# Chunked attention followed by a gated MLP: softmax weights written as block-diagonal 128x128 tiles, V products on the whole of TensorE in blocks 2 to 8

## The chip, the cores and the metric

The kernel runs on one core of a Trainium2 chip. The metric is the device time of one execution in microseconds (us), lower is better. Every comparison of times is between executions in the fast state (b_again, a single run whose state is unknown, serves for its profile alone), and a kernel is always timed in turns with the kernel before on the same chip. A ratio is the mean time of one kernel's fast runs over that of the other's of the same rounds, so it is not quite the ratio of the medians that are quoted beside it.

TensorE is written PE in the profile (PEld is its weight load), VectorE DVE, ScalarE ACT, GpSimd POOL and SyncE SP. A "q" after an engine's name is its instruction queue, for instance ACTq for a DMA that ScalarE issues.

## The reference, cut to what matters

```python
# q, k, v: (8, 8, 576, 64) float32; chunks of 64 tokens, 9 chunks per sequence
scores = (q_c @ k_c.transpose(...)) / sqrt(64)      # 64x64 per chunk and head
attn   = softmax(scores)
out    = attn @ v_c                                 # 64x64 @ 64x64
x      = out as (4608, 512)
h      = x @ w_in                                   # (512, 2048)
g      = h * sigmoid(beta * h)
result = g @ w_out                                  # (2048, 512)
```

The 4608 tokens are worked on in nine blocks of 512, numbered 0 to 8. Attention is 64x64 work per head and chunk; the two large products are 128x512 matmuls, 128 of them per block.

## The kernel before

All instructions are put into queues by a small scheduler: `at(time, function, ...)` gives an order, in slots of four 128x512 matmuls, and semaphores are derived from what is read and written. For blocks 2 to 8 the attention of the next block runs inside the w_out products (`mm2`) of the block before it. An attention starts at slot T, and the block's first w_in product (`mm1`) is at slot T + 16.

```python
def exp(blk, bank):                      # bank: a PSUM bank with 512 scores per partition
    dst, src = E[:, bank, :], A[:, bank, :]
    ...
    P.op("act", lambda e: e.activation(dst, src, AF.Exp, scale=0.125), ...)

def attend(blk, m, u, ps, bank):         # m: 128 tokens, u: half of the heads
    ...
    for h in range(4 * u, 4 * u + 4):
        for c2 in range(2):              # two chunks, two 64x64 quarters of TensorE
            r = slice(64 * c2, 64 * c2 + 64)
            ... e.matmul(ps[r, bank, 128 * (h % 4):128 * (h % 4) + 65],
                         E[r, e0 + h % 2, col:col + 64], vaug[r, m, h, 0:65])

def normalize(blk, m, us, ps, bank): ...  # DVE: reciprocal of column 64, then multiply, into x_sb
def turn_x(blk, m):                       # DMA transpose, issued by SyncE
    P.dma("sp", lambda e: e.dma_start_transpose(xT[:, :, 128 * m:128 * m + 128], x_sb[:, m, :]), ...)

def attention(blk, T):
    for u in range(2):
        at(T + 0.6, scores, blk, u)
    for i in range(4):
        at(T + 1 + 0.1 * i, exp, blk, i)
    for j in range(2):
        for m in (2 * j, 2 * j + 1):
            for u in range(2):
                at(T + 4.1 + 2.5 * j, attend, blk, m, u, A, 2 * (m % 2) + u)
            at(T + 4.2 + 2.5 * j, normalize, blk, m, (0, 1), A, 2 * (m % 2))
            at(T + 4.3 + 2.5 * j, turn_x, blk, m)
```

`mm1` reads all four turns (m = 0 to 3) of a block, so the last of them to land decides when a block's first w_in matmul can start.

The softmax here doesn't subtract the row's maximum and nothing guards it: scores larger than these inputs give would overflow.

## Time and profile before

| | before |
|---|---|
| median of the first three runs | 294.89 us (294.52 to 295.69) |
| span of the profiled execution | 293.6 us |
| PE / ACT / DVE / POOL busy | 96% / 51% / 48% / 25% |
| period from one block's scores to the next's | 29.95 us |

The first and the fourth part of the page of before: busy us and share of the span of each engine, and the chain of waits that ended last by engine.

```profile
PE 282.8 (96%) x2417; PEld 139.2 (47%) x2453; DVE 140.2 (48%) x231; ACT 148.4 (51%) x235; POOL 74.0 (25%) x109
PE 92%; DMA 2%; DVE 2%; ACT 2%; issue 1%; ACTq 0%; DVEq 0%
```

TensorE is busy 96% of the time, and 92% of the chain is TensorE. Matmuls are pipelined, so "busy" alone would not prove a limit; the chain does. Here is the chain of before through block 5, in order of time (start, length, what):

```profile
155.98 0.86 PE F L504 x4
156.84 0.74 PE A L394 x64
157.59 0.16 issue
157.75 3.40 PE F L504 x15
161.15 0.63 PE A L415 x32
161.78 0.54 PE F L504 x2
162.31 0.05 issue
162.37 1.24 PE F L504 x5
163.61 0.63 PE A L415 x32
164.24 2.70 PE F L504 x12
166.93 0.05 issue
166.99 5.13 PE F L504 x23
172.11 1.08 PE F L460 x5
```

L394 are the scores, L415 the V products, L504 w_out and L460 w_in. No other engine is on it. The short "issue" pieces come from matmul records that are missing in the trace (15 of 16, 7 of 8), not from waits. The timeline of TensorE in the same place:

```profile
159.69 1.46 PE L504 MATMUL F<-w_out_bf,g 128*128 128x512 bf16 x6
161.07 0.70 PE L415 MATMUL A<-vaug,E 64*64 64x65 bf16 x32
161.71 1.90 PE L504 MATMUL F<-w_out_bf,g 128*128 128x512 bf16 x7
```

A length in the timeline includes the tail of the last matmul. Costs below are therefore taken from start to start in the trace: 128x512 matmuls start every 0.2157 us. From the start of the last one ahead of a V burst to the start of the next one behind it is 0.94 us, so a burst costs 0.94 - 0.216 = 0.725 us, and two of them 1.45 us a block.

### The profile page before, as it was taken

What the parts mean: (1) busy time and instruction counts of PE and PEld (TensorE: products, weight loads), DVE (VectorE), ACT (ScalarE), POOL (GpSimd) and SP (SyncE); (2) the same over time, 40 slices, a digit from 0 to 9 for tenths busy, and PEclk for the clock granted to TensorE, in tenths of its full rate; (3) what the DMA queues carried; (4) which work ended last, traced back from release to release, by engine and by line L of the source; (5) the groups of instructions that cost most, each with busy time, mean ns of one, the idle gap of its engine ahead of it and who ended that gap; (6) DMA issues with size and microseconds to landing.
All of it is one profiled execution on the core that took longest, in us unless ns stands there. A gap on an engine that the chain in (4) does not pass through costs nothing.

```text
span 293.6 us, 5823 instructions
## 1 busy us (share of the span) xinstructions
PE 282.8 (96%) x2417; PEld 139.2 (47%) x2453; DVE 140.2 (48%) x231; ACT 148.4 (51%) x235; POOL 74.0 (25%) x109
## 2 busy tenths in 40 slices
PE   7799999999999999999999999999999999999994
PEld 3554456745444544454444444454444444544441
DVE  0657536784247333834373427442844175408600
ACT  2567425784167515851486057704861387137511
POOL 1346753514231503152032303230234000000000
PEclk9799999999999999999999999999999999999999
DMA  6999999999799959999998599959999920340033
GB/s 235 259 359 399 405 287 295 240 204 278 148 269 246 223 115 269 263 201 193 213 262 171 143 216 239 194 125 194 199 177 202 200 57 0 80 136 2 0 71 71
DMA packets 133497, 57.53 MB, mean 196 GB/s; under 512 B 116576, under 2 KB 124768, under 8 KB 133472
## 3 DMA queue, kind: packets, MB, share of 16 engines
q1 hardware_dynamic: 127872, 47.20, 72.7%
q10 hardware_dynamic: 5600, 9.97, 10.7%
q8 instruction: 19, 0.31, 0.5%
q14 instruction: 6, 0.05, 0.1%
HBM read 36.71 MB, written 9.44 MB: 157 GB/s over the span
## 4 chain that ended last, share of the span: by engine, by line
PE 92%; DMA 2%; DVE 2%; ACT 2%; issue 1%; ACTq 0%; DVEq 0%
PE F L504 42%; PE F L460 40%; PE A L415 3%; DMA kstage<-in_k_dram 2%; PE A L394 2%; PE F L480 1%; ACT tt L490 1%; PE F L452 1%; PE A L350 1%; PE F L350 1%; DVE kcast L266 0%; DVE x_sb L427 0%; PE F L443 0%; ACT xT L264 0%; PE F L415 0%
## 5 line engine op out<-in xcount | busy, mean ns | idle before, releaser
L472 DVE SCALAR_TENSOR_TENSOR g<-tt,F 128x512 bf16<-128x512 bf16 x136 | 93.4, 687 | 78.2 <-ACT tt L469 77.9
L504 PE MATMUL F<-w_out_bf,g 128*128 128x512 bf16 x550 | 127.2, 379 | 2.1 <-issue 1.1
L460 PE MATMUL F<-xT,w_in_bf 128*128 128x512 bf16 x534 | 118.2, 379 | 0.5
L469 ACT ACTIVATE tt<-F,beta_half 128x512 bf16<-128x512 f32 x136 | 93.5, 687 | 24.5 <-PE F L460 24.2
L504 PEld LDWEIGHTS F<-w_out_bf,g 128*128 128x128 bf16 x576 | 54.4, 98 | 63.0 <-POOL w_out_bf L266 0.2
L460 PEld LDWEIGHTS F<-xT,w_in_bf 128*128 128x128 bf16 x544 | 53.2, 98 | 64.0 <-DVE g L472 0.5
L512 ACT ACTIVATE ostage<-F 128x512 f32<-128x512 f32 x34 | 20.3, 597 | 88.6 <-PE F L504 88.2
L266 POOL CAST qcast<-qstage 128x1024 bf16<-128x1024 f32 (+1 forms) x18 | 17.0, 945 | 72.7 <-DMA qstage<-in_q_dram 72.7
L266 POOL CAST vaug<-vstage 128x512 bf16<-128x512 f32 x36 | 21.9, 613 | 47.8 <-DMA vstage<-in_v_dram 32.9
L427 DVE TENSOR_TENSOR x_sb<-A,rden 128x512 bf16<-128x512 f32 x34 | 23.5, 691 | 1.2
L266 POOL CAST kcast<-kstage 128x512 bf16<-128x512 f32 (+1 forms) x29 | 18.2, 628 | 23.2 <-DMA kstage<-in_k_dram 23.1
L425 DVE RECIPROCAL rden<-A 128x8 f32<-128x8 f32 x34 | 6.9, 202 | 35.2 <-PE A L415 35.2
L404 ACT ACTIVATE E<-A 128x512 bf16<-128x512 f32 x28 | 14.5, 603 | 4.4 <-PE A L394 4.4
L415 PEld LDWEIGHTS A<-vaug,E 64*64 64x64 bf16 x544 | 10.3, 108 | 6.9 <-ACT ostage L512 3.0
L415 PE MATMUL A<-vaug,E 64*64 64x65 bf16 x544 | 12.5, 193 | 0.0
L266 POOL CAST w_in_bf<-wstage 128x1024 bf16<-128x1024 f32 (+1 forms) x8 | 7.8, 987 | 5.5 <-DMA wstage<-in_moe_w_in_dram 5.5
L266 POOL CAST w_out_bf<-wstage 128x1024 bf16<-128x1024 f32 x8 | 8.1, 1041 | 2.1 <-DMA wstage<-in_moe_w_out_dram 2.1
L480 PE MATMUL F<-xT,w_in_bf 128*128 128x256 bf16 x64 | 7.9, 273 | 0.7 <-DVE xT L266 0.5
L490 ACT ACTIVATE tt<-F,beta_half 128x256 bf16<-128x256 f32 x16 | 6.4, 496 | 1.2 <-PE F L480 1.2
L494 DVE SCALAR_TENSOR_TENSOR g<-tt,F 128x512 bf16<-128x512 bf16 x8 | 5.5, 687 | 2.8 <-ACT tt L490 2.6
L266 DVE CAST qcast<-qstage 128x1024 bf16<-128x1024 f32 x2 | 1.9, 936 | 10.4 <-DMA qstage<-in_q_dram 10.4
L480 PEld LDWEIGHTS F<-xT,w_in_bf 128*128 128x128 bf16 x64 | 5.9, 98 | 1.7 <-DVE xT L266 0.9
(50 smaller groups left out, 68.8 us busy)
## 6 DMA issues: line engine op xcount, KB each, us to landing
vstage<-in_v_dram SPq DMA_DIRECT2D x32, 256.0 KB, 5.0
out_dram<-ostage ACTq DMA_DIRECT2D x32, 256.0 KB, 4.0
kstage<-in_k_dram SPq DMA_DIRECT2D x30, 256.0 KB, 7.1
qstage<-in_q_dram SPq DMA_DIRECT2D x12, 512.0 KB, 6.0
wstage<-in_moe_w_out_dram SPq DMA_DIRECT2D x4, 1024.0 KB, 14.5
qstage<-in_q_dram SPq DMA_DIRECT2D x8, 256.0 KB, 9.4
wstage<-in_moe_w_in_dram SPq DMA_DIRECT2D x4, 512.0 KB, 7.4
wstage<-in_moe_w_in_dram SPq DMA_DIRECT2D x2, 1024.0 KB, 11.8
```

Of the source, the lines that this page charges most:

```text
L266: P.op(eng, lambda e: e.tensor_copy(dst, src), reads=r, writes=wr)
L404: P.op("act", lambda e: e.activation(dst, src, AF.Exp, scale=0.125), reads=[K("A", bank, v=("s", blk))], writes=[K("E", bank, v=blk)])
L415: return e.matmul(ps[r, bank, 128 * (h % 4):128 * (h % 4) + 65], E[r, e0 + h % 2, col:col + 64], vaug[r, m, h, 0:65])
L425: P.op("dve", lambda e: e.reciprocal(rd, o[:, :, :, 64]), reads=r, writes=[K("rden", m, u, v=blk) for u in us])
L427: P.op("dve", lambda e: e.tensor_tensor(x_sb[:, m, 256 * us[0]:256 * (us[0] + n)].rearrange("p (b h d) -> p b h d", h=4, b=n), o[:, :, :, ...
L460: P.op("pe", lambda e, c=c: e.matmul(F[:, bank, :], w_in_bf[:, c, 256 * e0 + i:256 * e0 + 256:2], xT[:, c, :], start=(c == 0), stop=(c == ...
L469: P.op("act", lambda e: e.activation(tt[:, T % NTT, :], F[:, bank, :], AF.Tanh, scale=beta_half[:, e0, i:i + 1]), reads=[K("F", bank, v=(" ...
L472: P.op("dve", lambda e: e.scalar_tensor_tensor(g2[:, t, :], tt[:, T % NTT, :], 1.0, F[:, bank, :], ALU.add, ALU.mult), reads=[K("F", bank, ...
L480: P.op("pe", lambda e, i=i, c=c: e.matmul(F[:, bank, 256 * i:256 * i + 256], w_in_bf[:, c, 256 * pair + i:256 * pair + 256:2], xT[:, c, 25 ...
L490: P.op("act", lambda e, i=i: e.activation(tt[:, s, 256 * i:256 * i + 256], F[:, bank, 256 * i:256 * i + 256], AF.Tanh, scale=beta_half[:, ...
L504: P.op("pe", lambda e, t=t: e.matmul(F[:, s, :], g2[:, t, 128 * s:128 * s + 128], w_out_bf[:, t, :], start=(t == 0), stop=(t == NT - 1)), ...
L512: f = (lambda e: e.activation(dst, src, AF.Copy, scale=0.5)) if eng == "act" else \
```

## The change

The intent is to use all rows and columns of TensorE. exp writes the two 64x64 weights of two chunks onto the diagonal of a 128x128 tile whose other quarters were cleared once (in a staging buffer that is free by then). One 128x65 matmul then takes the place of two 64x65 matmuls in opposite quarters. Because exp must now write to different columns for the upper and lower 64 partitions, each exp covers 64 partitions by 1024 columns instead of 128 by 512. The schedule is changed with it: four bursts of 8 products, first half of the heads first, instead of two bursts of 32.

```diff
-        def exp(blk, bank):
-            dst, src = E[:, bank, :], A[:, bank, :]
+        EB = wstage[:, 0, :].bitcast(BF16).rearrange("k (g x) -> k g x", x=128)
+        def clear_E():
+            P.op("pool", lambda e: e.memset(EB, 0.0), ...)
+        def exp(blk, u, c2):
+            r = slice(64 * c2, 64 * c2 + 64)
+            dst = EB[r, 16 * u:16 * u + 16, 64 * c2:64 * c2 + 64]
+            src = A[r, 2 * u:2 * u + 2, :].rearrange("k b x -> k (b x)")
             ... 
+        def attend_pairs(blk, m, u, bank):
+            for h in range(4 * u, 4 * u + 4):
+                P.op("pe", lambda e, h=h: e.matmul(
+                    A[:, bank, 128 * (h % 4):128 * (h % 4) + 65],
+                    EB[:, 16 * u + 8 * (h % 2) + 4 * (h // 2 % 2) + m, :], vaug[:, m, h, 0:65]), ...)
             ...
-                at(T + 1 + 0.1 * i, exp, blk, i)
-            for j in range(2):
-                for m in (2 * j, 2 * j + 1):
-                    for u in range(2):
-                        at(T + 4.1 + 2.5 * j, attend, blk, m, u, A, 2 * (m % 2) + u)
-                    at(T + 4.2 + 2.5 * j, normalize, blk, m, (0, 1), A, 2 * (m % 2))
-                    at(T + 4.3 + 2.5 * j, turn_x, blk, m)
+                at(T + 1 + 0.1 * i, exp, blk, i // 2, i % 2)
+            for m, u, ta in ((0, 0, 3.9), (1, 0, 3.9), (2, 0, 5.2), (3, 0, 5.9), (0, 1, 6.2), (1, 1, 6.2),
+                             (2, 1, 8.1), (3, 1, 8.8)):
+                bank = 2 * u + m % 2
+                at(T + ta, attend_pairs, blk, m, u, bank)
+                at(T + ta + 0.01, normalize, blk, m, (u,), A, bank)
+                if u == 1:
+                    at(T + ta + 0.02, turn_x, blk, m)
             ...   # two loads of block 3 and the V loads of block 4 are queued a little later
+        at(40, clear_E)
```

More of the change, by code (lines that the diff above doesn't have):

```diff
@@ L397, in scores @@
                              writes=[K("A", bank, v=("s", blk))])
-        def exp(blk, bank):
-            dst, src = E[:, bank, :], A[:, bank, :]
+        EB = wstage[:, 0, :].bitcast(BF16).rearrange("k (g x) -> k g x", x=128)
+        def clear_E():
+            P.op("pool", lambda e: e.memset(EB, 0.0), writes=[K("ws", 0, e, v="E") for e in range(2)] +
+                 [K("EB", u, c2) for u in range(2) for c2 in range(2)])
+        def exp(blk, u, c2):
+            r = slice(64 * c2, 64 * c2 + 64)
+            dst = EB[r, 16 * u:16 * u + 16, 64 * c2:64 * c2 + 64]
+            src = A[r, 2 * u:2 * u + 2, :].rearrange("k b x -> k (b x)")
             if spread(blk):
-                dst = dst.rearrange("k (g p i) -> k g p i", p=16, i=4)
+                dst = dst.rearrange("k g (p i) -> k g p i", i=4)
                 src = src.rearrange("k (g i p) -> k g p i", p=16, i=4)
+            else:
+                src = src.rearrange("k (g x) -> k g x", x=64)
             P.op("act", lambda e: e.activation(dst, src, AF.Exp, scale=0.125),
-                 reads=[K("A", bank, v=("s", blk))], writes=[K("E", bank, v=blk)])
+                 reads=[K("A", 2 * u + i, v=("s", blk)) for i in range(2)], writes=[K("EB", u, c2, v=blk)])
+        def attend_pairs(blk, m, u, bank):
+            for h in range(4 * u, 4 * u + 4):
+                P.op("pe", lambda e, h=h: e.matmul(
+                    A[:, bank, 128 * (h % 4):128 * (h % 4) + 65],
+                    EB[:, 16 * u + 8 * (h % 2) + 4 * (h // 2 % 2) + m, :], vaug[:, m, h, 0:65]),
+                    reads=[K("EB", u, c2, v=blk) for c2 in range(2)] + [K("v", m, v=blk), K("ones")],
+                    writes=[K("A", bank, v=("o", blk, m, u))])
         def attend(blk, m, u, ps, bank):
@@ L552, in prepare @@
                 if blk == 3:
-                    lk[2:], ck[2:] = [55, 55.1], [55.5, 56.5]
+                    lk[2:], ck[2:] = [57.5, 57.6], [58, 58.5]
                 if blk == 4:
-                    lv = [87 + 0.1 * m for m in range(4)]
+                    lv = [89.5 + 0.1 * m for m in range(4)]
             for u in range(2):
```

## The prediction

> **What bounds the kernel now.** TensorE. The profile's first part gives it 96% busy; the chain of waits is 92% TensorE. From block 2 on the timeline repeats every 29.95 us without a stop: 128 matmuls of 128x512 at 0.2157 us (27.6 us) plus scores and V products. ScalarE is 51% busy, VectorE 48%.
>
> **What the change removes.** In blocks 2 to 8 the V products are two bursts of 32 matmuls on 64x64 quarters. By the timeline a burst is 0.70 us; from the start of the last 128x512 matmul before it to the start of the next after it is 0.94 us where 0.216 would pass without it. A burst costs 0.727 us, a block 1.45 us. About 0.2 us of each is the change of mode: 0.309 instead of 0.216 us going in, 0.124 instead of about 0.035 coming out. This agrees with the Trainium skill, "TensorEngine Tiling (Array Packing)", Key Properties: changing the tiling mode drains TensorE. The switch around the scores stays.
>
> **What it adds on TensorE.** 32 matmuls 128x65 per block, four bursts of 8, in the mode of their neighbours. No such shape is in the trace. The Trainium skill, "TensorE: Matmul & The Clock Gate", Back-to-back issue gap, gives N/2.4 + 2.5 ns; the trace agrees at N=512 (215.7 ns) and N=128 (transposes every 55.6 ns, each with its weight load). For N=65 that is 29.6 ns, an estimate. The weight load need not bind: after the switches two full loads start 15 ns apart. So 32 x 29.6 = 0.95 us a block, 0.51 us saved, 3.5 us over seven blocks. If a load bound at 55 ns, 2.2 us would be lost.
>
> **What it moves.**
> - exp: four of 64 partitions by 1024 columns instead of 128 by 512. 128x1024 ScalarE instructions take 1.02 us, so 4.1 instead of 2.06 us (timeline). First V products come 12 matmuls (2.6 us) after the scores, the second half's about 5.7 us after; both exps fit.
> - Normalize is in halves: eight pairs of about 0.57 us (estimate from 0.20 and 0.69).
> - The turn of x: the first can be issued only after the third burst, about 6.65 us after the scores instead of 4.77. The queue issues one per about 1.4 us, landing after 2.5 to 3.9 us. Today the last lands 2.0 to 2.3 us before the block's first w_in matmul. It moves 1.9 us later and the matmul 0.5 us earlier: slack becomes about -0.1 to -0.4 us. I expect TensorE to wait 0.25 us on average at each block's first w_in matmul, 1.75 us in all. This is new critical path, and the next output store may lengthen it.
> - A 128x4096 GpSimd memset (estimate 3.5 us from 0.204 for 128x128 and 0.098 for 128x1) delays block 2's K casts and V loads by about 2.5 us; that slack just suffices.
>
> **Time.** 294.9 - 3.5 + 1.75 = 293.1 us. 8 in 10: 291.0 to 295.6. Faster by over 2%: 0.04; within 2%: 0.93; slower by over 2%: 0.03.
>
> **What the profile would show.** Bursts of 8 at about 30 ns per start; normal spacing into and out of them. V products about 0.95 us a block. An idle time of TensorE of 0 to 0.5 us before the block's first w_in matmul, ended by the DMA writing xT. exps near 1.02 us. Block period about 29.7 us.
>
> **What would make it wrong.** Weight loads binding at 40 to 55 ns per product (saving gone). The last turn of x colliding with the output store (landing 3.9 us: 1 us wait per block, slower than before), or landing early (no wait, 291.4). Block 2 stalled by memset or late V. VectorE not freeing banks before the second or fourth burst.

## More of the kernel before

SyncE issues its DMAs in order: the loads of q, k and v share its queue with the turns. ScalarE issues the output stores.

## The result, and the profile after

The changed kernel took 295.68 us (median of 6, 294.99 to 296.42), the kernel before 294.98 us in the same rounds. The ratio is 1.0025 (95% interval 1.0004 to 1.0045): the gain did not appear, and the time lies just above the stated range. The table sets the forecast terms beside the profile.

| | before | after |
|---|---|---|
| V products a block, start to start | 1.450 us | 1.027 us |
| four exps of a block | 2.06 us | 4.14 us |
| last turn of x issued, after the scores begin (mean of blocks 2 to 8) | 10.13 us | 11.55 us |
| that turn, from issue to landing (mean) | 2.84 us | 3.45 us |
| landed, after the scores begin | 12.96 us | 15.00 us |
| wait of TensorE before the block's first w_in matmul, sum of blocks 2 to 8 | 0.00 us | 2.92 us |

A wait is the distance between the starts of the block's first w_in matmul and of the matmul ahead of it, less the usual 0.2157 us. It is larger than the idle time that the waits view shows, because there the modelled end of the matmul ahead counts as busy. (The expectations below that speak of 2.8 us left out the 0.15 us of block 2.)

The same two parts of the page of after, then the groups of the new V products and exps:

```profile
PE 282.6 (96%) x2229; PEld 138.4 (47%) x2229; DVE 147.3 (50%) x287; ACT 162.4 (55%) x235; POOL 77.2 (26%) x110
PE 82%; DMA 8%; SPq 3%; DVE 3%; issue 1%; ACT 1%; POOL 0%; ACTq 0%; POOLq 0%
L415 ACT ACTIVATE wstage<-A 64x1024 bf16<-64x1024 f32 x28 | 28.5, 1018 | 5.2 <-PE A L394 4.7
L420 PE MATMUL A<-vaug,wstage 128*128 128x65 bf16 x224 | 11.7, 194 | 0.0
```

TensorE's share of time is unchanged at 96%, but its share of the chain fell from 92% to 82%, and DMA and SyncE's queue came onto it. (The wstage in these names is the staging buffer in which the new tiles lie.) The chain of after through block 5:

```profile
157.78 0.74 PE A L394 x64
158.52 2.70 PE F L523 x12
161.22 0.25 PE A L420 x8
161.47 1.73 PE F L523 x8
163.20 0.26 PE A L420 x8
163.45 0.86 PE F L523 x4
164.32 0.26 PE A L420 x8
164.57 1.73 PE F L523 x8
166.30 0.14 PE A L420 x4
...
167.23 0.44 DVE x_sb L446
167.67 0.02 SPq L453
167.69 0.04 issue
167.73 1.26 SPq L453
168.99 0.04 issue
169.04 3.73 DMA xT<-x_sb
172.76 0.14 issue
172.90 1.24 PE F L479 x5
```

The bursts are as cheap as hoped: 0.25 us each, with no loss on either side. But the chain leaves TensorE in the fourth burst and goes through normalize, the queue and the last turn of x, which lands at 172.76 us. The w_in matmuls follow at 172.90, although TensorE had finished the w_out products before. The waits view of after, from 60 to 290 us, has these waits seven times, once for each block 2 to 8; in before there is no such line:

```profile
PEld F L479 <- issue: 5.0, 7, 1.0
PE F L479 <- DMA xT<-x_sb: 1.9, 5, 0.6
```

So 7 x (1.450 - 1.027) = 2.96 us were gained and 2.92 us given back in the profiled execution. The gain is a little larger than that: the second w_out matmul behind a quarter burst also comes late, 0.227 us after the first instead of 0.216, which this cost leaves out. Blocks without any wait (see e5_last_early) have a period of 29.49 us against 29.95, so 0.45 us a block, about 3.2 us in all, were saved.

The whole time from the scores of block 2 to the end of the span shows the same balance: 226.6 us in both profiles of before, 226.4 us in after and 226.7 in its repeat, a_again.

One more difference is in the profile of after: the scores of block 2 began at 67.98 us instead of 66.93, before any V product of the change. There the second of two early output stores took 2.57 us to issue on ScalarE and held up the next copy; this is taken up at b_again and e6.

### The profile page after: what moved, and what is told of

It reads as the page before. It is cut to its first block, busy times and chain, and to the rows that moved or that the text cites. A ratio compares the mean times of both kernels' runs of the same rounds, so it can differ in the third digit from the quotient of the medians.

```text
span 294.4 us, 5468 instructions
## 1 busy us (share of the span) xinstructions
PE 282.6 (96%) x2229; PEld 138.4 (47%) x2229; DVE 147.3 (50%) x287; ACT 162.4 (55%) x235; POOL 77.2 (26%) x110
## 4 chain that ended last, share of the span: by engine, by line
PE 82%; DMA 8%; SPq 3%; DVE 3%; issue 1%; ACT 1%; POOL 0%; ACTq 0%; POOLq 0%
PE F L479 40%; PE F L523 32%; DMA xT<-x_sb 6%; SPq L453 3%; PE F L499 3%; PE A L420 2%; DVE x_sb L446 2%; PE A L394 2%; DMA qstage<-in_q_dram 2%; PE F L350 1%; DVE rden L444 1%; PE A L350 1%; PE A L367 1%; SPq L333 1%; PE A L434 1%
## 5 line engine op out<-in xcount | busy, mean ns | idle before, releaser
L523 PE MATMUL F<-w_out_bf,g 128*128 128x512 bf16 x576 | 132.2, 379 | 0.0
L479 PEld LDWEIGHTS F<-xT,w_in_bf 128*128 128x128 bf16 x544 | 52.6, 98 | 67.6 <-issue 5.0
L523 PEld LDWEIGHTS F<-w_out_bf,g 128*128 128x128 bf16 x576 | 53.6, 98 | 59.1
L266 POOL CAST vaug<-vstage 128x512 bf16<-128x512 f32 x36 | 21.8, 613 | 49.5 <-DMA vstage<-in_v_dram 29.6
L415 ACT ACTIVATE wstage<-A 64x1024 bf16<-64x1024 f32 x28 | 28.5, 1018 | 5.2 <-PE A L394 4.7
L446 DVE TENSOR_TENSOR x_sb<-A,rden 128x256 bf16<-128x256 f32 (+1 forms) x62 | 27.9, 450 | 2.1
L444 DVE RECIPROCAL rden<-A 128x4 f32<-128x4 f32 (+1 forms) x62 | 11.2, 180 | 33.7 <-PE A L420 32.2
L420 PEld LDWEIGHTS A<-vaug,wstage 128*128 128x128 bf16 x224 | 10.8, 98 | 6.6
L420 PE MATMUL A<-vaug,wstage 128*128 128x65 bf16 x224 | 11.7, 194 | 0.0
L499 PEld LDWEIGHTS F<-xT,w_in_bf 128*128 128x128 bf16 x64 | 5.9, 98 | 1.8 <-DVE xT L266 0.9
```

The lines of the kernel that those rows point to most:

```text
L266: P.op(eng, lambda e: e.tensor_copy(dst, src), reads=r, writes=wr)
L420: P.op("pe", lambda e, h=h: e.matmul(A[:, bank, 128 * (h % 4):128 * (h % 4) + 65], EB[:, 16 * u + 8 * (h % 2) + 4 * (h // 2 % 2) + m, :], ...
L444: P.op("dve", lambda e: e.reciprocal(rd, o[:, :, :, 64]), reads=r, writes=[K("rden", m, u, v=blk) for u in us])
L446: P.op("dve", lambda e: e.tensor_tensor(x_sb[:, m, 256 * us[0]:256 * (us[0] + n)].rearrange("p (b h d) -> p b h d", h=4, b=n), o[:, :, :, ...
L479: P.op("pe", lambda e, c=c: e.matmul(F[:, bank, :], w_in_bf[:, c, 256 * e0 + i:256 * e0 + 256:2], xT[:, c, :], start=(c == 0), stop=(c == ...
L499: P.op("pe", lambda e, i=i, c=c: e.matmul(F[:, bank, 256 * i:256 * i + 256], w_in_bf[:, c, 256 * pair + i:256 * pair + 256:2], xT[:, c, 25 ...
```

## The experiments

All outputs are right. The middle columns are medians, the kernel before being timed in the same rounds. All ratios lie within 2% of 1. b_again, a single run of 295.61 us, is not in the table.

| run | median us | before, same rounds | ratio (95% interval) | sum of waits before w_in, profiled |
|---|---|---|---|---|
| after | 295.68 | 294.98 | 1.0025 (1.0004 to 1.0045) | 2.92 |
| a_again | 295.35 | 294.82 | 1.0017 (1.0000 to 1.0034) | 3.28 |
| e1_swap | 292.83 | 295.43 | 0.9918 (0.9898 to 0.9938) | 1.49 |
| e2_two_bursts | 295.90 | 295.43 | 1.0020 (0.9989 to 1.0051) | 0.00 |
| e3_quarters | 299.26 | 295.43 | 1.0136 (1.0108 to 1.0165) | 0.19 |
| e4_two_late | 293.69 | 294.82 | 0.9955 (0.9926 to 0.9984) | 0.42 |
| e4_again | 294.38 | 295.10 | 0.9976 (0.9951 to 1.0001) | 1.24 |
| e5_last_early | 292.23 | 294.82 | 0.9908 (0.9890 to 0.9927) | 0.03 |
| e6_stores_sp | 292.26 | 294.82 | 0.9910 (0.9893 to 0.9927) | 0.31 |
| e7_store_late | 292.79 | 295.10 | 0.9923 (0.9911 to 0.9936) | 1.39 |

### e1_swap: finish the first half of x earlier

```diff
-  ((0, 0, 3.9), (1, 0, 3.9), (2, 0, 5.2), (3, 0, 5.9), (0, 1, 6.2), (1, 1, 6.2), (2, 1, 8.1), (3, 1, 8.8))
+  ((0, 0, 3.9), (1, 0, 3.9), (0, 1, 5.2), (1, 1, 5.9), (2, 0, 6.2), (3, 0, 6.2), (2, 1, 8.1), (3, 1, 8.8))
```

> The changed kernel with its second and third bursts of V products exchanged, so that both head halves of the first two 128-row groups of x are finished after the second burst; nothing else differs. Theory A (the gain of the full-array V products, about 0.43 us a block, is given back because the last turn of x lands after TensorE is ready for the block's first w_in matmul, 0.1 to 0.7 us a block, 2.8 us in all in the profile of after): the first turn is issued about 1.1 us earlier relative to the scores, the wait before the first w_in matmul goes to zero, the period of a block becomes 29.52 us, and the time falls by about 2.8 us against after, to 292.2 to 293.2 us. Rival B (the turns only wait behind something that limits them anyway, the queue or the DMA engines, so that an earlier issue lands no earlier): wait and time stay, 295.2 to 296 us.

The time fell to 292.83 us, in theory A's range: 0.8% below before, where after and a_again are 0.2% above it, which is 2.9 to 3.2 us apart by the ratios. The first turn is issued 6.33 us after the scores begin instead of 7.44, and five of the seven blocks have no wait at all: their period is 29.50 us. The forecast of no wait anywhere failed in two blocks: 0.27 us in block 3 and 1.22 us in block 7. In block 7 the first turn was issued at 7.47 us, behind eight V loads of the last block that SyncE had to issue first. The queue view of SyncE in e1_swap shows it:

```profile
213.61 7.54 SPq L287 DMA_DIRECT2D vstage<-in_v_dram  x8
221.20 6.89 SPq L453 DMA_TRANSPOSE xT<-x_sb  x4
```

x_sb was ready about one us before 221.20 by the distance in the other blocks. One exchange in the order of work, with no instruction added or taken away, brings back what the products had gained. Rival B falls.

### e2_two_bursts: the new products in the old schedule

```diff
-            for m, u, ta in (...four bursts...)
+            for j in range(2):
+                for m in (2 * j, 2 * j + 1):
+                    for u in range(2):
+                        at(T + 4.1 + 2.5 * j, attend_pairs, blk, m, u, 2 * (m % 2) + u)
+                    at(T + 4.2 + 2.5 * j, normalize, blk, m, (0, 1), A, 2 * (m % 2))
+                    at(T + 4.3 + 2.5 * j, turn_x, blk, m)
```

> Full-array V products and block-diagonal exps, but in the schedule of before: two bursts of 16, both halves normalized at once. It asks whether the new schedule of four bursts was needed. Theory A: the last exp ends about 4.0 us after the scores (four of 1.02 us) but the first burst is due after 16 matmuls, 3.45 us, so TensorE waits about 0.6 us a block for ScalarE, 4 us in all; there is no wait for xT, since the first turn comes at about 5.5 us. 296 to 297.5 us. Rival B (exp length is off the critical path): as fast as 292 to 293 us.

295.90 us, just under theory A's range. The first burst breaks in two. The timeline of TensorE in e2_two_bursts:

```profile
161.81 0.29 PE L420 MATMUL A<-vaug,wstage 128*128 128x65 bf16 x4
162.41 0.56 PE L420 MATMUL A<-vaug,wstage 128*128 128x65 bf16 x12 [0.32 <-ACT wstage L415]
162.81 1.89 PE L523 MATMUL F<-w_out_bf,g 128*128 128x512 bf16 x8
```

The two bursts together cost 1.51 us start to start (the record of the first w_out matmul behind the second burst is missing, for which 0.216 us are taken off), of which 1.02 are products, so 0.49 us a block is waiting for the last exp. No block waits for xT. The period is 29.98 us, 0.49 above the 29.49 of blocks without any wait; that it is nearly before's 29.95 is a coincidence of two terms. So the longer exps are harmless only where a later or split first burst hides them: the old schedule would not have done, but after's order of bursts was not needed either, as e1_swap shows.

### e3_quarters: the schedule and exps of after, the products of before

```diff
-                P.op("pe", lambda e, h=h: e.matmul(
-                    A[:, bank, 128 * (h % 4):128 * (h % 4) + 65],
-                    EB[:, 16 * u + 8 * (h % 2) + 4 * (h // 2 % 2) + m, :], vaug[:, m, h, 0:65]),
+                for c2 in range(2):
+                    r = slice(64 * c2, 64 * c2 + 64)
+                    P.op("pe", lambda e, h=h, r=r: e.matmul(
+                        A[r, bank, 128 * (h % 4):128 * (h % 4) + 65],
+                        EB[r, 16 * u + 8 * (h % 2) + 4 * (h // 2 % 2) + m, r], vaug[r, m, h, 0:65]),
```

> The changed kernel with its schedule, exps and block-diagonal tiles, but the V products again as two 64x64 quarters each, reading the diagonal blocks. It separates the full-array products from everything else that the change did. Theory A: four bursts of 16, each with a change of mode of about 0.2 us and 0.26 us of products, so about 1.87 us a block instead of 1.02; the w_in matmul comes later, so the wait for xT shrinks from 0.4 to 0.1 us on average: plus 3.5 to 4 us against after, 299 to 300 us. Rival B (V products are not what sets the block's period in after, the chain exp, normalize, turn does): within 0.5 us of after.

299.26 us, 3.6 us above after by the medians and 3.3 by the ratios, inside theory A's range. It also shows what the full-array product gains. The timeline of TensorE in e3_quarters, around the first burst:

```profile
160.70 1.67 PE L525 MATMUL F<-w_out_bf,g 128*128 128x512 bf16 x7
162.30 0.44 PE L422 MATMUL A<-vaug,wstage 64*64 64x65 bf16 x16
162.68 1.90 PE L525 MATMUL F<-w_out_bf,g 128*128 128x512 bf16 x8
```

A burst of 16 quarter products costs 0.468 us start to start (in three of the four bursts of a block; behind the second a matmul record is missing), a burst of 32 in before 0.725. So 16 more, or 8 more pairs, cost 0.257 us: 32 ns a pair. One full-array 128x65 product also takes 32 ns (8 in 0.256 us). The products themselves are equally fast. What remains of a quarter burst is 0.468 - 0.256 = 0.21 us, in both lengths measured, and this is the whole gain: two such costs a block are 0.42 us, against 0.423 measured start to start. At the edges, in before, the first quarter product starts 0.309 us after the last full one instead of 0.216, and the next full one 0.124 us after the last pair instead of 0.032.

### b_again and a_again: both kernels unchanged

> The kernel before, unchanged, for a second profile. In the profile of after the kernel is 1.05 us later than before already at the scores of block 2, before anything of the change is on the critical path: the issue of the second early output store on ScalarE's queue took 2.57 us there and 0.44 us before, and held up the copy of block 1's keys. Theory C (chance of the DMA queues from run to run): this second profile of before may show an issue of 0.4 to 2.6 us too, and the scores of block 2 between 66.9 and 68 us. Theory D (something that comes with the change): it shows 0.44 us and 66.9 us again.

> The changed kernel unchanged, for a second profile and more times beside the others. Theory A: the waits of TensorE before the first w_in matmul of blocks 2 to 8 sum to 2 to 3.5 us again (2.8 in the first profile), and the V products cost 1.02 us a block. If the 1.05 us of the first 68 us was chance, the profile's scores of block 2 lie anywhere between 66 and 68 us; 294.7 to 296 us.

In b_again the store's issue took 0.44 us, and the scores of block 2 began at 67.17 us. In a_again, whose instructions are those of after, it also took 0.44 us, and the scores began at 66.45 us. So the changed kernel is not bound to have the delay. Of the eleven profiles with these stores on ScalarE, two (after and e2_two_bursts) have it; that the kernel before can have it too is not shown, since neither of its two profiles does. Over all twelve profiles the scores of block 2 start between 65.97 and 67.98 us. a_again's waits sum to 3.28 us, and its V products cost 1.03 us a block, as theory A has it.

### e4_two_late and e4_again: two bursts, late enough for the exps

```diff
-                        at(T + 4.1 + 2.5 * j, attend_pairs, blk, m, u, 2 * (m % 2) + u)
+                        at(T + 5.1 + 2.5 * j, attend_pairs, blk, m, u, 2 * (m % 2) + u)
```

with the same shift of normalize and turn_x, against e2_two_bursts.

> Two bursts of 16 full-array products as in e2_two_bursts, but 4 matmuls later, so that the exps are done. Theory A: no wait for ScalarE and none for xT (last turn issued about 10.7 us after the scores begin, landing before 14.4, needed at 14.73): period 29.52 us, 292.3 to 293.3 us, like e1_swap. It would say that the count of bursts costs nothing in the full-array mode. Rival: if small bursts had their own cost, it is faster than e1_swap by more than 0.5 us.

> e4_two_late again: its six times lay between 291.8 and 294.6 us, although its profile shows only one wait of 0.42 us. If its slack (0.9 to 1.7 us in that profile) is eaten in some executions by DMA traffic, a profile of a slower execution shows waits of TensorE before the first w_in matmul of several blocks, ended by the DMA that writes xT; if the spread comes from the first 68 us, the scores of block 2 start later than 67 us and the periods stay 29.49 us.

Two bursts of 16 cost 1.021 us a block, four of 8 1.027: the count of bursts costs nothing in the full-array mode. But the times missed the range: 293.69 and 294.38 us, with single runs from 291.8 to 295.2. The two profiles show a wait of 0.42 us in block 7 in one, and 0.97 us in block 2 and 0.27 us in block 6 in the other, where the start was also late (scores of block 2 at 67.82 us instead of 66.70). These two differences, 0.82 and 1.12 us, are nearly the whole 2.0 us between the two profiled spans. The last turn is issued 10.71 and 10.90 us after the scores begin on average, hardly later than the 10.62 us of e5_last_early, so that alone does not explain why these runs scatter more. The cause of the scatter is left open.

### e5_last_early: the remaining waits of e1_swap

```diff
-  (2, 1, 8.1), (3, 1, 8.8)
+  (2, 1, 7.1), (3, 1, 7.1)
+                if blk == B:
+                    lv = [T - 23.5 + 0.1 * m for m in range(4)]      # V loads behind block 7's turns
```

> e1_swap with the fourth burst 4 to 8 matmuls earlier and the V loads of the last block put behind the turns of block 7 on the queue. In e1_swap's profile two waits remained, 0.27 us in block 3 and 1.22 us in block 7, where the first turn was issued 1.15 us late behind eight V loads. Theory A: last turn issued at about 9.5 us instead of 10.7, block 7's first at 6.3 instead of 7.5; no wait left in any block; 0.3 to 1.5 us below e1_swap, 291.5 to 292.6 us. Rival (the DMA engines and not the order on the queue hold block 7): its wait stays near 1 us and the time within 0.4 us of e1_swap.

292.23 us, ratio 0.9908: the lowest of all, 2.6 us ahead of before, which after did not beat. The first turn of block 7 is issued at 6.32 us and the one wait left is 0.03 us in block 2. In the waits view TensorE no longer waits for xT. So the forecast of the waits was right, and the rival, which had block 7 wait near 1 us, falls. The time is in the range too, but e1_swap ran on another chip, and by their ratios the two are only 0.1% (0.3 us) apart with overlapping intervals: that e5_last_early is the faster of the two is not shown.

### e6_stores_sp: the early stores on another queue

```diff
-                    at(28 if early else 32 * blk + 16 + n, store, blk, s)
+                    at(40.5 if early else 32 * blk + 16 + n, store, blk, s, *(["sp"] if early else []))
```

> e5_last_early with the two early output stores issued by SyncE later instead of by ScalarE before the copy of block 1's keys. In the profiles of after and e2_two_bursts the second of these issues took 2.6 and 2.9 us and delayed that copy by about 1 us; in the four others 0.44 us and no delay. Theory C (chance, in any kernel of this family): this kernel never shows the delay, from the quarter-turn of block 0 to the scores of block 2 takes the same as in the undelayed profiles, and its mean time is 0.2 to 0.7 us below e5_last_early. Rival: no difference, or slower because the stores hold up the turns of block 2's queries.

292.26 us against 292.23: no difference. So no gain on average from removing the rare delay on ScalarE's queue is shown, and since a_again is as slow as after without it, it does not explain after's time. The ACT queue of after and of before, where it was seen and not seen:

```profile
44.82 2.57 ACTq L538 DMA_DIRECT2D out_dram<-ostage  x1
47.44 1.02 ACT L264 ACTIVATE kT<-A 128x1024 bf16<-128x1024 bf16 x1 [2.07 <-DVE x_sb L446]
```

```profile
44.60 0.87 ACTq L519 DMA_DIRECT2D out_dram<-ostage  x2
46.32 1.02 ACT L264 ACTIVATE kT<-A 128x1024 bf16<-128x1024 bf16 x1 [0.68 <-PE A L350]
```

The profile puts the idle time of the copy down to VectorE, because that is the last semaphore that it saw; the instruction just ahead in the queue is what held it.

### e7_store_late: take the output store away from the last turn

```diff
-                    at(28 if early else 32 * blk + 16 + n, store, blk, s)
+                    at(28 if early else 32 * blk + 16 + n + (4.5 if s == 2 and 0 < blk < B - 1 else 0), store, blk, s)
```

against after, with its order of bursts. By the edit these are the stores of blocks 1 to 6, not 1 to 7 as the expectation says.

> The changed kernel with one thing moved: in blocks 1 to 7 the third output store is issued after the fourth instead of 3.5 us before it, so that it no longer shares the DMA engines with the last turn of x. In both profiles of after the last turn takes about 3.45 us to land (2.84 in before), and in block 5 the store filled the engines from 171.0 to 171.9 us, inside that turn's 169.0 to 172.8. Theory E (the turn's lateness in issue uses up the slack, and the collision with the store makes the wait 0.4 us instead of my 0.25 or less): landing falls to 2.5 to 3.0 us, the wait per block from 0.40 to 0.0 to 0.15 us, the time by 1.5 to 2.7 us against after: 292.8 to 294.2 us. Rival (loads and the next query turn on the other queue make it slow): landing and waits as in after, 295 to 296 us.

292.79 us, at the lower edge of theory E's range. The last turns of blocks 2 to 7 now land 2.47 to 2.53 us after issue instead of 3.10 to 3.73. Six blocks have waits of 0.06 us in sum; block 7 has 1.34 us, with its first turn issued late behind V loads as in e1_swap. DMA queues while the last turn of block 5 was under way, in after and in e7_store_late (q1 is SyncE's queue, q10 ScalarE's with the stores; packets, MB, share of 16 engines):

```profile
q1 hardware_dynamic: 1858, 0.46, 64.0%
q10 hardware_dynamic: 144, 0.26, 23.5%
xT<-x_sb SPq DMA_TRANSPOSE x1, 3.7
```

```profile
q1 hardware_dynamic: 1087, 0.26, 52.5%
xT<-x_sb SPq DMA_TRANSPOSE x1, 2.5
```

The transpose of the next block's q is under way on q1 in both. With the 0.26 MB store out of the way the turn lands 1.2 us sooner. In before it was the store ahead of this one (issued at 165.87 us) that met the last two turns of block 5: the third took 3.9 us to land and the fourth 3.0, yet the fourth had slack enough.

## Why the prediction was wrong

- What bounds the kernel, and what a burst of quarter products costs, was right. 0.2 us for each change of mode was confirmed by e3_quarters at 0.21 us. The Trainium skill, "TensorEngine Tiling (Array Packing)", Key Properties, says that changing the tiling mode drains TensorE. These runs agree in that a visit to the quarter mode has a fixed cost, and show that the change's gain is this cost alone and not the larger tile; that it is the drain is the page's explanation and was not tested further.
- 29.6 ns a product, from the formula of the Trainium skill, "TensorE: Matmul & The Clock Gate", Back-to-back issue gap, was 8% low: the products start 29 to 35 ns apart, 32.0 on average. (That section itself says that the formula under-counts at small N.) The saving is 3.0 us by the bursts and 3.2 by the periods, instead of 3.5. The weight loads did not bind at 55 ns.
- exp at 1.02 us was right (1.018), and so was the memset: 3.51 us by the trace, with no wait in block 2 for it.
- The step that failed is the last one of "what it moves": "I expect TensorE to wait 0.25 us on average at each block's first w_in matmul, 1.75 us in all." The mechanism is right, as e1_swap and e5_last_early show. The sizes were off. The slack in before, 2.0 to 2.4 us and 2.20 on average, was eaten by four terms: last turn issued 1.42 us later (11.55 - 10.13), landing 0.61 us longer (3.45 - 2.84), matmul wanted 0.45 us earlier, and 0.14 us from the landing to the matmul's start (the "issue" piece at 172.76 in the chain). They sum to 2.62 us, which leaves the wait of 0.42 us. I allowed for 1.9, nothing, 0.5 and nothing. The landing time was taken from before and carried over, although the turn moved to a time when an output store is on the DMA engines; the text names that collision only as a possibility and gives it no time. That the issue was forecast too late hid part of this: by luck, the sum came nearer than its terms. The wait came to 0.42 us a block in one profile and 0.47 in the other, 2.92 and 3.28 us in all, instead of 1.75.
- The sum: -3.2 + 2.9 or 3.3 gives -0.3 or +0.1 us for the part of the kernel that the change touches, where I had forecast -1.75 and the medians of the whole show +0.7 and +0.5. So 1.2 to 1.5 us of the miss are the wait and 0.3 us the saving. The rest, 0.4 to 1.0 us, lies in the first 68 us or in scatter (the scores of block 2 start within 2.0 us of each other over twelve profiles) and is not explained further.

With the waits taken away, the expected gain is there: in e5_last_early the time from the scores of block 2 to the end is 223.5 us, 3.2 less than in before, and the median is 2.6 us lower.

## What to carry to other kernels

A saving on the engine that bounds the kernel counts only as far as everything it waits for has slack. Add up how much earlier the engine will want its input and how much later that input will now start, and compare the sum with the slack in the trace. A DMA's time to land belongs to its moment as much as to its size, so look at what the other queues will carry when it moves. When an item of work must be complete before a slow transfer can start, order the work so that the first item is finished first, rather than the first half of all items.

## What the Trainium skill lacked or had wrong

- "TensorEngine Tiling (Array Packing)", Key Properties: it gives no figure for the drain at a change of tiling mode. Here a visit to the 64x64 mode cost 0.21 us beyond its products, start to start, for bursts of 16 and of 32 alike (0.468 and 0.725 us).
- "TensorEngine Tiling (Array Packing)", Theoretical Speedup: it is silent on the case in which the small products can be put on a diagonal. Here two 64x65 products in opposite quarters and one 128x65 product both took 32 ns, weight load included.
- "TensorE: Matmul & The Clock Gate", Back-to-back issue gap: it gives 81 ns for a pair of weight load and matmul at N=128 and 131 ns at N=512 as sustained values, and calls N/2.4 + 2.5 ns the isolated gap. In this kernel the latter holds for pairs at N=128 (55 to 56 ns) and N=512 (215.7 ns); at N=65 it is 32.0 ns against 29.6.
- "DMA: Bandwidth & Descriptors", DMA Transpose (X-bar): it has no time for one small transpose. Turns of 128x512 bf16 within SBUF took 1.2 to 2.5 us each on SyncE's queue and at best 2.4 us from issue to landing. With a 0.26 MB store beside it the last turn took 3.45 us on average instead of 2.5.
- "Perfetto Trace Analysis", DMA Instruction — HWDGE (DVE, Sync): it gives no time for how long issuing a DMA holds the engine that issues it. Here the issue of the second early store on ScalarE took 0.44 us in nine of eleven profiles and 2.57 and 2.86 us in two.
